# Moving the weight loads, the loads of batch 2 and the second products at the start of a fused attention and MLP kernel

## The chip, the cores and the metric

The kernel runs on one core of a Trainium2 chip. The metric is the device time of one execution in microseconds (us), as the median of several runs. A profile of one execution comes with each kernel; times inside a profile are counted from its span's start.

## The reference

Linear attention per head (`kv = k^T v`, `out = q kv`, RMS norm over the head's 64 columns), then an MLP with an ELU. Inputs and output are float32.

```python
def _attn_ref(q, k, v, g_norm):               # q, k, v: (8, 8, 576, 64)
    kv = np.einsum('bhsd,bhse->bhde', k, v)
    out = np.einsum('bhsd,bhde->bhse', q, kv)
    rms = np.sqrt(np.mean(out * out, axis=-1, keepdims=True) + 1e-06)
    return (out / rms * g_norm).astype(np.float32)

def _moe_ref(x, w_in, w_out):                 # x: (4608, 512), w_in: (512, 2048), w_out: (2048, 512)
    h = x @ w_in
    g = np.where(h > 0.0, h, np.exp(np.minimum(h, 0.0)) - 1.0)
    return (g @ w_out).astype(np.float32)
```

## The kernel before

The rows are worked through in nine groups of 512. For group T the kernel makes `xT` (attention, norm, transposes), then in eight steps the first products `h_ps = xT . w_in` and the ELU into `gT`, then the second products `o_ps = gT . w_out` in sixteen "quarters" of four matmuls of 128x512 (a "half" is two quarters). While group T's products run, the attention of batch T+1 is woven in as "pieces". From group 2 on the pattern is regular. The change concerns the start: groups 0 and 1, and what is loaded for them.

Three queues start transfers: SyncE (`nc.sync`), ScalarE (`nc.scalar`) and GpSimd (`nc.gpsimd`). The weights are turned from float32 to bf16 by the DMA itself. The Trainium skill, "DMA: Bandwidth & Descriptors", section "SWDGE vs HWDGE vs iDMA", says that a cast during DMA has to be issued from GpSimd; that is why the change moves the weights within GpSimd's queue and not to another one.

```python
def fetch(b, eng=nc.sync):                     # float32 staging tiles st_q, st_k, st_v, one buffer each
    fetch_q(b, eng)
    for name, src in (("k", k), ("v", v)):
        out_, in_ = fetch_kv(name, src, b)
        eng.dma_start(out=out_, in_=in_)

def load_w_in(s):  nc.gpsimd.dma_start(out=w_in_sb[...], in_=...)     # a quarter of w_in, cast to bf16
def load_w_out(s): nc.gpsimd.dma_start(out=w_out_sb[...], in_=...)    # a quarter of w_out
# ... cast_q, cast_kv: GpSimd copies st_* to bf16 tiles, which frees the staging buffer

def mm1(T, i, cols, relu, spare):              # ... cut: 8 matmuls into h_ps
    nc.scalar.activation(e, h_ps, AF.Exp)      # ScalarE
    if relu: nc.scalar.activation(h, h_ps, AF.Relu)
    def rest():                                # VectorE: min/subtract, then max (or add, with relu) into gT
        ...
    return rest

# pieces of attention(T): kv, q (transposes of q), se0/se1 (q . kv into PSUM, then squares on ScalarE),
# sum0/1 (VectorE), inv0/1 (ScalarE), mul0/1 (VectorE, scales the rows: xs), x (transposes of xs into xT)
# All of kv, q, se0, se1 and x share one PSUM tile `at`: se1 can start only when mul0 has read se0.

fetch(1)
for s in range(2): load_w_in(s)
cast_q(1, Q)
for s in range(2, 4): load_w_in(s)
cast_kv("k", 1, Q)
cast_kv("v", 1, Q)
for s in range(4): load_w_out(s)

def first_products(T, at, second, start, relu=(), spare=()):
    # for each step i: mm1; the early pieces (sum, inv); second[i](); rest(); the late pieces
    ...

at = attention(1)
at["fetch"] = lambda: fetch(2, nc.scalar)
start = {"q": 1, "kv": 4, "se0": 5, "fetch": 6, "se1": 7}
first_products(0, at, {}, start, (1, 3, 5, 7), (2, 5))
mm2_half(0, 0)
mm2_half(0, 1)
at["x"]()
mm2_half(0, 2)
cast_all(2)
fetch(3)
at = attention(2)
second = {i: (lambda i=i: mm2_quarter(0, 6 + i)) for i in range(8)}
start = {"q": 1, "kv": 2, "se0": 3, "se1": 5, "x": 7}
first_products(1, at, second, start, (1, 3, 5, 7))
mm2_half(0, 7)
# ... groups 2 to 8, unchanged
```

## Time and profile before

| | before |
|---|---|
| time, median of the first 4 runs | 320.69 us (320.2 to 321.54) |
| profiled execution, span | 317.4 us |
| TensorE busy | 299.1 us, 94% |
| ScalarE / VectorE / GpSimd busy | 49% / 56% / 21% |

The first fence is the head of the profile's page. The profiled execution itself took 319.24 us, 1.45 us less than the median of the four. TensorE (PE) is busy nearly all the time, and in the timeline it has no gap left after about 80 us. So a change to the start is worth what it takes out of TensorE's gaps and slow stretches before that.

```profile
span 317.4 us, 4742 instructions
...
PE 299.1 (94%) x1941; PEld 150.4 (47%) x1941; DVE 179.3 (56%) x217; ACT 156.5 (49%) x218; POOL 66.3 (21%) x117
```

The next fence is the timeline of TensorE near the end of group 0: start, length, engine, line, operation, and in brackets how long the engine was idle before and what ended that.

```profile
42.80 0.77 PE L187 MATMUL at<-bd_kv,qT 128*128 128x128 bf16 x8 [2.73 <-DVE xs L221]
43.36 4.32 PE L360 MATMUL o_ps<-w_out_sb,gT 128*128 128x512 bf16 x12
48.48 1.02 PE L360 MATMUL o_ps<-w_out_sb,gT 128*128 128x512 bf16 x4 [0.80 <-DMA w_out_sb<-in_moe_w_out_dram]
51.20 1.05 PE L281 MATMUL at<-ident,xs 128*128 128x128 bf16 x16 [1.70 <-DVE xs L221]
```

L187 is the attention product se1, L360 second products, L281 the transposes of xs. There are three gaps: 2.73 us until the first row scaling (mul0), 0.80 us until the last part of w_out, 1.70 us until the second row scaling (mul1). Why mul1 is so late is told by ScalarE's timeline:

```profile
40.33 0.21 ACT L218 ACTIVATE ss<-ss 128x16 f32<-128x16 f32 x1
40.42 0.98 ACTq L83 DMA_DIRECT2D st_q<-in_q_dram  x2
41.49 0.46 ACTq L112 DMA_DIRECT2D st_k<-in_k_dram  x1
42.05 3.10 ACTq L112 DMA_DIRECT2D st_v<-in_v_dram  x1
45.20 1.02 ACT L327 ACTIVATE elu_e<-h_ps 128x1024 bf16<-128x1024 f32 x1 [4.65 <-issue]
...
47.02 1.03 ACT L206 ACTIVATE sq<-at 128x1024 bf16<-128x1024 f32 x1
```

ACTq is ScalarE's queue issuing DMA. It issues batch 2's q, k and v at 40.4 us, and the issue of v alone takes 3.10 us. The exponential of step 7 starts only at 45.20 us, 4.65 us after ScalarE's last work, and the squares that mul1 depends on come behind it, at 47.02 us.

The last view is busy time in windows of 2 us. A line has the window and its length, then busy time (and count of instructions) of PE, PEld (the weight loads of TensorE), DVE (VectorE), ACT (ScalarE) and POOL (GpSimd). The columns that matter are the last three: PEclk, the granted clock of TensorE (1.00 is full), DMA share (over 1 is a full DMA) and GB/s written. For the weights, which the DMA turns from 4 bytes to 2, the bytes read are twice those written.

```profile
32.00:34.00 2.00, 2.00 (x36) 1.22 (x36) 1.79 (x4) 2.00 (x3) 2.00 (x5) 1.00 0.24 32
40.00:42.00 2.00, 0.08 (x1) 0.00 (x0) 1.90 (x3) 0.52 (x2) 0.00 (x0) 1.00 1.24 206
42.00:44.00 2.00, 1.20 (x10) 0.86 (x10) 0.75 (x1) 0.00 (x0) 0.00 (x0) 0.78 1.24 205
44.00:46.00 2.00, 2.00 (x6) 0.68 (x5) 0.00 (x0) 0.81 (x1) 0.00 (x0) 0.50 1.17 245
```

At 32 to 34 us the DMA is nearly empty, because w_out has only just been issued. After the 2.73 us gap the clock is half for 3.4 us, and the 12 matmuls at 43.36 take 4.32 us instead of 2.6.

### The profile page before, as it was taken

How to read it: one execution, taken by the hardware profiler on the slowest of the kernel's cores; microseconds unless marked ns; L12 is line 12 of the kernel's file. 1: busy time of each engine (PE TensorE's matmuls, PEld its weight loads, DVE VectorE, ACT ScalarE, POOL GpSimd, SP SyncE). 2: the span in 40 equal slices, each digit the busy share in tenths (PEclk: the TensorE clock that was granted, in tenths of full speed). 3: DMA queues.
4: the chain of work that ended last, by engine and by line, in shares of the span. 5: the costliest groups of instructions: out<-in, count | busy, mean ns of one | idle time of the engine just before them, and what ended most of it. 6: DMA issues, size and time to landing. Idle time of an engine off the chain costs nothing.

```text
span 317.4 us, 4742 instructions
## 1 busy us (share of the span) xinstructions
PE 299.1 (94%) x1941; PEld 150.4 (47%) x1941; DVE 179.3 (56%) x217; ACT 156.5 (49%) x218; POOL 66.3 (21%) x117
## 2 busy tenths in 40 slices
PE   8778966998999999999999999999999999999993
PEld 3444523553554545454545454545454545444441
DVE  4565744578448744774487458745774676554400
ACT  3556933667445454545554555445544555334220
POOL 0246405950045005400540063002000000000000
PEclk9999979999999999999999999999999999999999
DMA  7999799920491049105810591034101010101122
GB/s 256 316 290 253 121 238 387 363 99 2 138 355 71 0 148 348 69 0 168 328 67 2 158 340 66 0 108 94 68 0 66 2 66 2 66 0 66 68 66 66
DMA packets 28565, 42.24 MB, mean 133 GB/s; under 512 B 5504, under 2 KB 17792, under 8 KB 28544
## 3 DMA queue, kind: packets, MB, share of 16 engines
q1 hardware_dynamic: 22208, 34.35, 31.4%
q0 software_dynamic: 4224, 4.19, 8.1%
q10 hardware_dynamic: 2112, 3.41, 3.0%
q8 instruction: 15, 0.25, 0.3%
q14 instruction: 6, 0.05, 0.0%
HBM read 36.70 MB, written 9.44 MB: 145 GB/s over the span
## 4 chain that ended last, share of the span: by engine, by line
PE 80%; DMA 8%; DVE 4%; ACT 4%; ACTq 1%; POOL 0%; issue 0%; SPq 0%; DVEq 0%
PE o_ps L360 36%; PE h_ps L318 35%; DMA w_in_sb<-in_moe_w_in_dram 5%; PE at L165 2%; PE at L281 2%; DMA st_v<-in_v_dram 2%; PE at L175 2%; PE at L187 2%; ACT elu_e L327 1%; DVE gT L344 1%; DVE ss L211 1%; ACTq L112 1%; DVE xs L221 1%; ACT elu_h L331 1%; ACT sq L206 1%; DVE elu_e L336 1%
## 5 line engine op out<-in xcount | busy, mean ns | idle before, releaser
L360 PE MATMUL o_ps<-w_out_sb,gT 128*128 128x512 bf16 x576 | 137.0, 382 | 0.8 <-DMA w_out_sb<-in_moe_w_out_dram 0.8
L318 PE MATMUL h_ps<-xT,w_in_sb 128*128 128x512 bf16 (+1 forms) x584 | 135.6, 376 | 1.7 <-DMA w_in_sb<-in_moe_w_in_dram 1.7
L327 ACT ACTIVATE elu_e<-h_ps 128x1024 bf16<-128x1024 f32 (+1 forms) x74 | 74.0, 1001 | 67.2 <-PE h_ps L318 62.6
L360 PEld LDWEIGHTS <-gT 128*128 128x128 bf16 x576 | 56.7, 99 | 69.3 <-issue 3.2
L336 DVE TENSOR_SCALAR elu_e<-elu_e 128x1024 bf16<-128x1024 bf16 (+1 forms) x73 | 35.6, 487 | 94.1 <-ACT elu_e L327 94.1
L318 PEld LDWEIGHTS <-w_in_sb 128*128 128x128 bf16 x584 | 55.2, 98 | 61.4 <-DMA w_in_sb<-in_moe_w_in_dram 2.2
L344 DVE TENSOR_TENSOR gT<-elu_e,h_ps 128x1024 bf16<-128x1024 bf16 (+1 forms) x65 | 78.3, 1205 | 6.8
L130 POOL CAST q_bf<-st_q 128x512 bf16<-128x512 f32 x32 | 19.3, 640 | 136.1 <-DMA st_q<-in_q_dram 92.3
L370 ACT COPY o_sb<-o_ps 128x512 f32<-128x512 f32 x36 | 21.1, 586 | 24.9 <-PE o_ps L360 24.9
L206 ACT ACTIVATE sq<-at 128x1024 bf16<-128x1024 f32 (+1 forms) x18 | 17.5, 981 | 13.7 <-PE at L187 11.1
L130 POOL CAST v_bf<-st_v 128x512 bf16<-128x512 f32 (+1 forms) x36 | 20.8, 620 | 12.5 <-DMA st_v<-in_v_dram 12.0
L211 DVE TENSOR_REDUCE ss<-sq 128x16 f32<-128x1024 bf16 x16 | 19.5, 1219 | 4.8 <-ACT sq L206 4.5
L130 POOL CAST k_bf<-st_k 128x512 bf16<-128x512 f32 (+1 forms) x35 | 19.6, 604 | 7.8 <-DMA st_k<-in_k_dram 7.8
L221 DVE TENSOR_TENSOR xs<-at,ss 128x1024 bf16<-128x1024 f32 x16 | 19.5, 1218 | 0.6 <-ACT ss L218 0.6
L291 ACT ACTIVATE xT<-at,g_col 128x1024 bf16<-128x1024 bf16 x8 | 8.9, 1114 | 19.0 <-DVE xT L288 19.0
L421 PE MATMUL idle_ps<-zeros,ident 128*128 128x512 bf16 x45 | 13.3, 434 | 1.4 <-POOL ident masks.py:199 1.4
L250 ACT COPY qT<-at 128x1024 bf16<-128x1024 bf16 x8 | 8.1, 1012 | 9.4 <-DVE qT L249 9.4
L187 PE MATMUL at<-bd_kv,qT 128*128 128x128 bf16 x120 | 9.3, 221 | 3.3 <-DVE xs L221 3.3
L187 PEld LDWEIGHTS <-qT 128*128 128x128 bf16 x128 | 8.5, 98 | 7.2 <-issue 3.9
L165 PE MATMUL at<-v_bf,k_bf 64*128 64x128 bf16 x288 | 9.8, 216 | 2.0 <-DVE v_bf L130 1.1
L165 PEld LDWEIGHTS <-k_bf 64*128 64x128 bf16 x288 | 8.3, 94 | 5.9 <-issue 4.8
L281 PE MATMUL at<-ident,xs 128*128 128x128 bf16 x128 | 8.4, 219 | 2.3 <-DVE xs L221 2.3
(46 smaller groups left out, 105.3 us busy)
## 6 DMA issues: line engine op xcount, KB each, us to landing
out_dram<-o_sb SPq DMA_DIRECT2D x16, 512.0 KB, 2.6
st_q<-in_q_dram SPq DMA_DIRECT2D x14, 512.0 KB, 5.5
st_k<-in_k_dram SPq DMA_DIRECT2D x6, 1152.0 KB, 8.7
st_v<-in_v_dram SPq DMA_DIRECT2D x6, 1152.0 KB, 10.9
w_in_sb<-in_moe_w_in_dram POOLq DMA_DIRECT2D x4, 512.0 KB, 13.0
w_out_sb<-in_moe_w_out_dram POOLq DMA_DIRECT2D x4, 512.0 KB, 9.4
st_k<-in_k_dram SPq DMA_DIRECT2D x2, 576.0 KB, 6.8
st_v<-in_v_dram SPq DMA_DIRECT2D x2, 576.0 KB, 7.8
```

The costliest lines, as they stand in the source:

```text
L130: eng.tensor_copy(out=out_, in_=in_)
L165: nc.tensor.matmul(kv_ps[s][:, u * P : u * P + P], lhsT=bf["k", T][rows, j, 2 * u : 2 * u + 2, :], rhs=bf["v", T][rows, j, 2 * u : 2 * u + ...
L187: nc.tensor.matmul(ov[:, u, :, s, :], lhsT=qT[:, p, j * P : j * P + P], rhs=bd_kv[:, T, p, :], start=True, stop=True,)
L206: nc.scalar.activation(sq, se_ps, AF.Square)
L211: nc.vector.reduce_sum(out=ss, in_=sq.rearrange("p c (h e) -> p (c h) e", h=H), axis=AX.X)
L221: nc.vector.tensor_tensor(out=xs.rearrange("p c (h e) -> p (c h) e", h=H), in0=se_ps.rearrange("p c (h e) -> p (c h) e", h=H), in1=ss.to_b ...
L318: nc.tensor.matmul(h_ps[a][:, cs], lhsT=w_in_sb[:, c, f * P : f * P + P], rhs=x[:, c, cs], start=(c == 0), stop=(c == KC - 1),)
L327: nc.scalar.activation(e[:, lo:hi, :], ps, AF.Exp)
L336: nc.vector.tensor_scalar(out=e[:, lo:hi, :], in0=e[:, lo:hi, :], scalar1=1.0, scalar2=1.0, op0=ALU.min, op1=ALU.subtract,)
L344: nc.vector.tensor_tensor(out=gT[T][:, 2 * i + lo : 2 * i + hi, :], in0=e[:, lo:hi, :], in1=h, op=ALU.add if relu else ALU.max,)
L360: nc.tensor.matmul(o_ps[T, j], lhsT=gT[T][:, f, j * P : j * P + P], rhs=w_out_sb[:, f, :], start=(f == 0), stop=(f == FC - 1),)
L370: nc.scalar.copy(o_sb[T][:, j % 2, :], o_ps.pop((T, j)))
```

## The change

The intent: keep the DMA full by queuing all weight loads early; take the load issues away from ScalarE, which is needed at that time; but keep batch 2 from competing with the weights, by a tiny DMA on SyncE (the "gate") that reads a piece of `gT` written by the last ELU of group 0, so that all that SyncE issues after it waits for that ELU; and rearrange the second products in quarters, and the steps that use relu on ScalarE, to cover the waits.

```diff
     fetch(1)
-    for s in range(2):
+    for s in range(4):
         load_w_in(s)
     cast_q(1, Q)
-    for s in range(2, 4):
-        load_w_in(s)
+    for s in range(4):
+        load_w_out(s)
     cast_kv("k", 1, Q)
     cast_kv("v", 1, Q)
-    for s in range(4):
-        load_w_out(s)
...
+    def hold_loads():
+        gate = const.tile([1, 64], BF16, name="gate")
+        nc.sync.dma_start(out=gate, in_=gT[0][0:1, FC - 1, 0:64])
+
     at = attention(1)
-    at["fetch"] = lambda: fetch(2, nc.scalar)
-    start = {"q": 1, "kv": 4, "se0": 5, "fetch": 6, "se1": 7}
-    first_products(0, at, {}, start, (1, 3, 5, 7), (2, 5))
-    mm2_half(0, 0)
-    mm2_half(0, 1)
+    start = {"q": 1, "kv": 4, "se0": 5, "se1": 7}
+    first_products(0, at, {}, start, (2, 3, 6), (2, 5))
+    hold_loads()
+    fetch(2)
+    cast_all(2)
+    for i in range(5):
+        mm2_quarter(0, i)
     at["x"]()
-    mm2_half(0, 2)
-    cast_all(2)
+    mm2_quarter(0, 5)
     fetch(3)
     at = attention(2)
-    second = {i: (lambda i=i: mm2_quarter(0, 6 + i)) for i in range(8)}
+    quarters = iter(range(6, 16))
+    counts = (0, 1, 1, 1, 2, 1, 1, 1)            # quarters woven into step i
+    second = {...}                               # cut
     start = {"q": 1, "kv": 2, "se0": 3, "se1": 5, "x": 7}
-    first_products(1, at, second, start, (1, 3, 5, 7))
-    mm2_half(0, 7)
+    first_products(1, at, second, start, (1, 3, 4, 6))
+    for i in quarters:
+        mm2_quarter(0, i)
```

More of the change, by code (lines that the diff above doesn't have):

```diff
@@ L551, in first_products @@
                 at[name]()
+    def hold_loads():
+        gate = const.tile([1, 64], BF16, name="gate")
+        nc.sync.dma_start(out=gate, in_=gT[0][0:1, FC - 1, 0:64])
     at = attention(1)
-    at["fetch"] = lambda: fetch(2, nc.scalar)
-    start = {"q": 1, "kv": 4, "se0": 5, "fetch": 6, "se1": 7}
-    first_products(0, at, {}, start, (1, 3, 5, 7), (2, 5))
-    mm2_half(0, 0)
-    mm2_half(0, 1)
+    start = {"q": 1, "kv": 4, "se0": 5, "se1": 7}
[5 more added lines that the diff above has]
+        mm2_quarter(0, i)
     at["x"]()
-    mm2_half(0, 2)
-    cast_all(2)
+    mm2_quarter(0, 5)
     fetch(3)
     at = attention(2)
-    second = {i: (lambda i=i: mm2_quarter(0, 6 + i)) for i in range(8)}
+    quarters = iter(range(6, 16))
+    counts = (0, 1, 1, 1, 2, 1, 1, 1)
+    second = {
+        i: (lambda n=n: [mm2_quarter(0, next(quarters)) for _ in range(n)])
+        for i, n in enumerate(counts)
+    }
     start = {"q": 1, "kv": 2, "se0": 3, "se1": 5, "x": 7}
-    first_products(1, at, second, start, (1, 3, 5, 7))
-    mm2_half(0, 7)
+    first_products(1, at, second, start, (1, 3, 4, 6))
+    for i in quarters:
+        mm2_quarter(0, i)
     for T in range(2, NT):
```

## The prediction

It was written before the changed kernel was built or run.

> **What bounds the kernel now.** TensorE is busy 299.1 of 317.4 us (page, part 1). In the chain of work it is solid from about 80 to 312 us, so only idle or slow TensorE time before 80 us can be won. The timeline of TensorE shows the gaps after the first product starts: 1.17 us at 27.9 (w_in slice), 2.73 at 42.8 (row scaling on DVE), 0.80 at 48.5 (w_out), 1.70 at 51.2 (row scaling), later 0.23, 0.58, 0.58: 7.8 us. The windows also show a granted clock of 0.5 from 43.1 to 46.5 us, after the 2.73 us gap: 12 matmuls took 4.3 us instead of 2.6, so 1.7 us more. The Trainium skill, "TensorE: Matmul & The Clock Gate" (Part 1), says that an idle window halves the clock for about 3.4 us; the trace agrees (3.4 us).
>
> **What the change does.**
> 1. Batch 2's loads leave ScalarE, which issues them from 40.4 to 45.2 us (one issue alone 3.1 us), so that step 7's exponential, the squares and the second row scaling (49.9 to 51.2 us) come late. From the trace's durations I work out: step 7's exponential ends at 41.6, first scaling 42.4 (relu on step 6 saves DVE 0.5 us; 0.35 us earlier than now), step 7's ELU 44.1, sums 45.3, second scaling 47.1. The 1.70 us gap goes.
> 2. Weights earlier. GpSimd issues w_out at 32.5 to 35.5 us and the DMA is nearly empty at 32 to 34 us (0.15 to 0.33, windows). Queued at 19.4 they follow w_in without a hole; at 205 GB/s, as weights move alone (windows 28 to 31, 41 to 43), w_out (2.1 MB written) lands by about 44 instead of 48.5 us. The 0.80 us gap goes. Batch 1's loads should not suffer: the weight queue was never empty before 32 us, and is served in order. Four issues of 0.75 us fit into GpSimd's 3.2 us idle before the cast of k.
> 3. Batch 2 is issued on SyncE only at about 44.1 us, 3.7 us later, but on free DMA (387 GB/s, 8.8 us plus latency): v lands near 56 us as now (56.2), casts end near 59. The kv product wants it at 57.6 to 59: little or no stall.
> 4. Five quarters before the transposes cover the second scaling; the one after is 0.5 to 0.7 us too short for xT's two copies (0.75, then 1.1 us). In group 1, two quarters at step 4 cover the gap before the second attention product; the gap before the transposes stays, and step 7 without relu adds about 0.5 us on DVE before xT.
>
> **Sum.** The first gap only shrinks to 2.4 us, and the half clock probably stays. Group 1's first product ends near 53.1 instead of 55.7: 2.6 us. With full clock 4.2, but then v's cast limits it to about 3. Plus 0.8 us in group 1, minus 0.5 at its end: 3.2 us in all, 1%.
>
> **Predicted: 317.5 us, 80% range 315.5 to 319.8.** Faster by over 2%: 0.06; within 2%: 0.91; slower by over 2%: 0.03.
>
> **What would show it.** No ScalarE issue gap at 40 to 45 us; w_out issued at 19 to 22.5 us; no DMA hole at 32 to 34; the gap before group 0's transposes gone; TensorE still idle about 2.4 us before 42.5 and at half clock after; v of batch 2 cast by about 59; TensorE solid from about 77 us.
>
> **What would make it wrong.** A full weight queue that blocks GpSimd, so that k and v of batch 1 are cast late and the kv product stalls (several us slower); batch 2 landing after 57 us, so that group 1 stalls at its q or kv product; a clock that stays full with v early (gain over 4 us).

## The result, and the profile after

| | before | after |
|---|---|---|
| time, first measurement (4 runs each) | 320.69 us | 315.82 us (315.7 to 317.1), ratio 0.9854, 95% interval 0.9821 to 0.9887 |
| time, second measurement (11 and 6 runs) | 319.95 us | 316.57 us (315.83 to 318.02), ratio 0.9902, interval 0.9868 to 0.9936 |
| span of the first profile | 317.4 us | 313.9 us |
| TensorE's last product ends | 312.0 us | 308.0 us |

A ratio is the mean time of one kernel's fast runs over that of the other's of the same rounds, so it is not quite the ratio of the medians quoted. The gain is 4.9 us in one measurement and 3.4 us in the other, 1.0% to 1.5%: clear of noise, since neither interval reaches 1. Both intervals leave room for the same gain, near 0.987 to 0.989, and the second reaches up to 0.994.

The page's head, and the same stretch of TensorE, now:

```profile
span 313.9 us, 4706 instructions
...
PE 295.2 (94%) x1905; PEld 149.7 (48%) x1941; DVE 179.5 (57%) x217; ACT 155.4 (50%) x217; POOL 67.1 (21%) x117
```

```profile
42.31 0.61 PE L187 MATMUL at<-bd_kv,qT 128*128 128x128 bf16 x8 [2.18 <-DVE xs L221]
42.76 4.48 PE L360 MATMUL o_ps<-w_out_sb,gT 128*128 128x512 bf16 x19
47.13 1.05 PE L281 MATMUL at<-ident,xs 128*128 128x128 bf16 x16
48.02 1.03 PE L360 MATMUL o_ps<-w_out_sb,gT 128*128 128x512 bf16 x4
49.03 0.59 PE L318 MATMUL h_ps<-xT,w_in_sb 128*128 128x512 bf16 x2
50.17 3.18 PE L318 MATMUL h_ps<-xT,w_in_sb 128*128 128x512 bf16 x14 [0.55 <-ACT xT L291]
...
57.94 0.51 PE L165 MATMUL at<-v_bf,k_bf 64*128 64x128 bf16 x12 [0.23 <-ACT qT L250]
58.70 1.08 PE L165 MATMUL at<-v_bf,k_bf 64*128 64x128 bf16 x24 [0.25 <-POOL v_bf L130]
```

The wait for w_out and the 1.70 us gap before the transposes are gone. The first gap is 2.18 instead of 2.73 us. The 19 matmuls at 42.76 us (one record is missing) take 4.48 us, full speed. Small waits show at three places: 0.55 us for xT's second copy, which is new, and 0.23 and 0.25 us at the kv product of group 1. The first of these (for the transposes of q) was there before with the same 0.23 us; the second, for the cast of batch 2's v, is new. Group 1's first product starts at 49.0 us instead of 53.8.

ScalarE goes straight from the piece inv0 (L217 and L218) to step 7's exponential:

```profile
40.61 0.22 ACT L218 ACTIVATE ss<-ss 128x16 f32<-128x16 f32 x1
40.73 1.01 ACT L327 ACTIVATE elu_e<-h_ps 128x1024 bf16<-128x1024 f32 x1
42.96 1.02 ACT L206 ACTIVATE sq<-at 128x1024 bf16<-128x1024 f32 x1 [1.22 <-PE at L187]
45.27 0.31 ACT L217 ACTIVATE ss<-ss,eps_col 128x16 f32<-128x16 f32 x1 [1.29 <-DVE ss L211]
```

The windows:

```profile
32.00:34.00 2.00, 2.00 (x34) 1.18 (x34) 1.13 (x3) 2.00 (x4) 1.33 (x2) 1.00 1.24 207
40.00:42.00 2.00, 0.13 (x1) 0.00 (x0) 1.90 (x3) 1.70 (x4) 0.00 (x0) 1.00 1.19 197
42.00:44.00 2.00, 1.69 (x14) 1.03 (x14) 1.82 (x3) 1.02 (x1) 0.00 (x0) 1.00 0.27 47
44.00:46.00 2.00, 1.95 (x11) 0.88 (x10) 1.36 (x2) 0.52 (x2) 0.00 (x0) 1.00 0.08 8
```

At 32 to 34 us the DMA is full; at 42 to 46 us it is almost empty, because the weights are done and batch 2 is held. The clock is full throughout. SyncE's queue shows the gate and, behind it, the first load of batch 2:

```profile
43.95 0.58 SPq L554 DMA_DIRECT2D gate<-gT  x1
44.65 1.06 SPq L83 DMA_DIRECT2D st_q<-in_q_dram  x2
```

### The profile page after: what moved, and what is told of

Read it like the earlier page. It is cut to its first block, busy times and chain, and to the rows that moved or that the text cites. A ratio compares the mean times of both kernels' runs of the same rounds, so it can differ in the third digit from the quotient of the medians.

```text
span 313.9 us, 4706 instructions
## 1 busy us (share of the span) xinstructions
PE 295.2 (94%) x1905; PEld 149.7 (48%) x1941; DVE 179.5 (57%) x217; ACT 155.4 (50%) x217; POOL 67.1 (21%) x117
## 4 chain that ended last, share of the span: by engine, by line
PE 78%; DMA 8%; DVE 5%; ACT 3%; POOL 2%; issue 2%; SPq 1%; DVEq 0%; POOLq 0%
PE o_ps L360 36%; PE h_ps L318 34%; DMA w_in_sb<-in_moe_w_in_dram 4%; DVE gT L344 2%; DMA st_k<-in_k_dram 2%; DMA st_v<-in_v_dram 2%; PE at L165 2%; PE at L281 2%; PE at L187 2%; PE at L175 2%; ACT elu_e L327 1%; DVE elu_e L336 1%; POOL v_bf L130 1%; POOL k_bf L130 1%; DVE xs L221 1%
## 5 line engine op out<-in xcount | busy, mean ns | idle before, releaser
L318 PE MATMUL h_ps<-xT,w_in_sb 128*128 128x512 bf16 (+1 forms) x564 | 133.7, 376 | 3.6 <-DMA w_in_sb<-in_moe_w_in_dram 1.7
L360 PE MATMUL o_ps<-w_out_sb,gT 128*128 128x512 bf16 x562 | 134.4, 379 | 0.8
L344 DVE TENSOR_TENSOR gT<-elu_e,h_ps 128x1024 bf16<-128x1024 bf16 (+1 forms) x66 | 79.5, 1205 | 6.9
L130 POOL CAST k_bf<-st_k 128x512 bf16<-128x512 f32 (+1 forms) x35 | 20.7, 636 | 7.7 <-DMA st_k<-in_k_dram 7.7
L421 PE MATMUL idle_ps<-zeros,ident 128*128 128x512 bf16 x43 | 12.4, 422 | 1.6 <-POOL ident masks.py:199 1.4
L241 ACT CAST bd_kv<-at 64x256 bf16<-64x256 f32 x14 | 5.2, 369 | 9.8 <-PE at L165 9.7
```

What stands on the lines that cost most here:

```text
L130: eng.tensor_copy(out=out_, in_=in_)
L318: nc.tensor.matmul(h_ps[a][:, cs], lhsT=w_in_sb[:, c, f * P : f * P + P], rhs=x[:, c, cs], start=(c == 0), stop=(c == KC - 1),)
L344: nc.vector.tensor_tensor(out=gT[T][:, 2 * i + lo : 2 * i + hi, :], in0=e[:, lo:hi, :], in1=h, op=ALU.add if relu else ALU.max,)
L360: nc.tensor.matmul(o_ps[T, j], lhsT=gT[T][:, f, j * P : j * P + P], rhs=w_out_sb[:, f, :], start=(f == 0), stop=(f == FC - 1),)
```

## The experiments

The parts of the change are called A (weights early), B (batch 2 on SyncE behind the gate) and C (the rest: relu steps, quarters, and where `cast_all(2)` stands). "Theory 1" is the prediction's: the gain comes from ScalarE being freed, that is from B. Twelve runs follow, eleven kernels and the changed kernel once more, in three calls (on chips 3, 15 and 3); each call has its own runs of the kernel before, and the ratios are to those. All gave correct results.

### Each part alone

**a_weights_early** is the kernel before with the first hunk of the diff only.

> Only the weight loads move (all four of w_in, then all four of w_out, ahead of the casts of k and v); batch 2 stays on ScalarE, products and relu stay. Theory 1 (the gain comes from ScalarE no longer issuing batch 2): w_out lands by about 44 us and the 0.80 us wait on it goes, but the transposes of group 0 still wait for the second row scaling at about 51 us, so the gap there grows from 1.70 to about 2.5 us and the time stays at 320.7 within 0.6. Rival 1 (weights were what mattered): 1 us or more faster, 319.7 or less.

Measured: 317.06 us (316.67 to 318.17) against 319.72, ratio 0.9914 (0.9886 to 0.9942). Theory 1 fails here: it said no gain, and 2.7 us came. But so does the simple rival, since the 0.80 us that TensorE waited for w_out cannot give 2.7 us. ScalarE's timeline shows the reason:

```profile
40.39 0.99 ACTq L83 DMA_DIRECT2D st_q<-in_q_dram  x2
41.47 0.46 ACTq L112 DMA_DIRECT2D st_k<-in_k_dram  x1
42.03 0.50 ACTq L112 DMA_DIRECT2D st_v<-in_v_dram  x1
42.58 1.02 ACT L327 ACTIVATE elu_e<-h_ps 128x1024 bf16<-128x1024 f32 x1 [2.05 <-issue]
```

The same four DMA issues on the same engine at the same time now take 2.05 us: the issue of v took 0.50 us instead of 3.10. Step 7's exponential runs at 42.58 instead of 45.20, and the transposes follow at 48.58 instead of 51.20. So moving the weights on GpSimd shortened a stall on ScalarE.

**b_held_sync** is the kernel before with `hold_loads(); fetch(2)` after the first products, and without the fetch on ScalarE.

> Only batch 2's loads move, from ScalarE to SyncE behind the gate; weights late and halves as before. Theory 1: ScalarE has no issue gap, the second row scaling ends near 47.1 us instead of 51.2, and 2.5 to 4 us are gained: 317 to 318.2. Rival 1 (weights): at most 1 us, since w_out still lands after 46 us and holds the second products. Rival 2 (the gain is the clock that stays full): the time follows the granted clock, 319 or more if a half-clock stretch shows after the gap near 42 us.

Measured: 317.3 us (316.96 to 317.51), ratio 0.9913 (0.9884 to 0.9942), within the expectation. Alone, B is worth as much as A (2.4 and 2.7 us). ScalarE has no issue gap, and of the 1.70 us wait for mul1 0.21 us are left:

```profile
48.54 1.05 PE L281 MATMUL at<-ident,xs 128*128 128x128 bf16 x16 [0.21 <-DVE xs L221]
```

Rival 2, the clock, finds no support: this profile has no half-clock stretch, and the run with the lowest mean clock (0.984) took 316.97 us, less than the median.

**c_reorder** is the changed kernel with the old weight order and with `fetch(2, nc.scalar)` at step 6.

> Only the relu steps and the quarters change; weights late, batch 2 on ScalarE at step 6. Theory 1: the second row scaling moves by the 0.9 us that step 7 no longer spends on relu, to about 50.2 us; five quarters fill more of the wait; 0.5 to 1.5 us faster (319.2 to 320.2). Rival 3 (the order of relu and quarters is the main thing): 2.5 us or more faster.

Measured: 319.17 us (318.78 to 321.0), ratio 0.9984 (0.9951 to 1.0016): 0.6 us by the medians, not clear of noise. In its profile mul1 ends at 50.97 us and not at the 50.2 that I expected: ScalarE is stopped for 4.48 us, v's issue takes 2.93 us, and TensorE waits 1.25 us for w_out and 0.68 us for mul1.

### Two parts together

If A and B removed different waits, 0.9914 times 0.9913 would give 0.983 for both. A stall that both shorten would give less.

**ab_no_reorder**: the first hunk, and b_held_sync's edit.

> Weights early and batch 2 held on SyncE, but relu and halves as before. If the two moves removed different waits, their gains (2.7 and 2.4 us alone) would add to 5.1 us, a ratio near 0.984. Theory now (weights early alone already shortens ScalarE's issue stall from 4.65 to 2.05 us, so both moves shorten the same stall): at most 4 us, a ratio of 0.987 to 0.990; the transposes of group 0 start near 47.5 us with a gap of about 0.7 us before them.

Measured: 317.24 us (316.62 to 317.3) against 320.94, ratio 0.9884 (0.9862 to 0.9906). The product of the two is outside the interval, so the gains overlap. (The product is itself uncertain, by about 0.003 to either side when the runs are resampled, and comes from another chip; it stays below the measured ratio all the same. The table below shows the overlap in the profiles.) The transposes start at 47.86 us after a gap of 0.76 us.

**bc_weights_late**: the changed kernel with the old weight order.

> The changed kernel with the weights queued as late as before. Overlap theory: ScalarE's stall is gone all the same; the fourth quarter waits for w_out until about 47 us and the transposes move from 47.1 to about 48.5; ratio 0.988 to 0.991 (about 1 to 1.5 us slower than the changed kernel). If the weights' move were worth its 2.7 us here too: ratio 0.994.

Measured: 316.9 us, ratio 0.9882 (0.986 to 0.9905), as the overlap theory said. TensorE waits 0.55 us for w_out, and the transposes start at 48.16 us.

**ac_fetch_act**: the changed kernel without `hold_loads(); fetch(2)` and with the fetch on ScalarE at step 6.

> The changed kernel with batch 2's loads back on ScalarE at step 6. Overlap theory: with w_out done by about 42.5 us the issue of v no longer blocks (0.5 us instead of 3.1), ScalarE loses about 2 us, the second scaling ends near 48.5, a gap of 1 to 1.5 us before the transposes; batch 2 is some 3 us earlier, so no wait at the kv product of group 1; ratio 0.986 to 0.990. If the 3.1 us issue belongs to ScalarE whatever the DMA does: a stall of 4.5 us and a ratio of 0.994 or more.

Measured: 316.83 us, ratio 0.9877 (0.9853 to 0.9901). ScalarE is stopped for 2.06 us and v's issue takes 0.50 us, as expected from the overlap:

```profile
43.48 0.50 ACTq L112 DMA_DIRECT2D st_v<-in_v_dram  x1
44.03 1.02 ACT L327 ACTIVATE elu_e<-h_ps 128x1024 bf16<-128x1024 f32 x1 [2.06 <-issue]
```

The gap of 1 to 1.5 us before the transposes did not show, because this profile has a half-clock stretch that slowed the quarters until mul1 was ready.

The three kernels with two parts gained 3.7 to 4.1 us by the medians. The changed kernel, with all three, gained 4.9 and 3.4 us. It was run at another time. So the times do not show that the third part adds anything. The profiles suggest it: the transposes start 0.7 to 2.8 us earlier with all three (table), part of which is how late the run started.

This table is worked out from the profiles: the time from the end of mul0 to the end of mul1 (which leaves out by how much the start of the run was late), and what stopped ScalarE.

| kernel | ScalarE stopped by issues | v's issue | mul0's end to mul1's end | transposes start | span |
|---|---|---|---|---|---|
| before | 4.65 us | 3.10 us | 8.39 us | 51.20 | 317.4 |
| C | 4.48 | 2.93 | 8.69 | 51.03 | 317.0 |
| A | 2.05 | 0.50 | 5.80 | 48.58 | 314.9 |
| A and C | 2.06 | 0.50 | 6.42 | 49.89 | 315.9 |
| B | 0 | on SyncE | 4.82 | 48.54 | 315.6 |
| A and B | 0 | on SyncE | 4.81 | 47.86 | 314.9 |
| B and C | 0 | on SyncE | 4.81 | 48.16 | 314.7 |
| the change | 0 | on SyncE (0.45) | 4.81 | 47.13 | 313.9 |

The floor is 4.81 us. B alone takes off the whole 3.6 us above it, A alone 2.6 us. So once A is there, B has about 1 us of this stall left to give; once B is there, A has none of it left, only the wait for w_out (0.39 us in B's profile, 0.55 in that of B and C). The transposes start 4.07 us earlier after the change, and 3.6 us of that is this one stall, which two of its parts attack; the rest is the earlier end of mul0 (0.5 us).

Why did v's issue take 3 us? The trace counts packets by queue. In the kernel before, the first packet of ScalarE's queue starts at 44.0 us, 3.6 us after its first issue, and until then the weights' queue is at its full 205 GB/s; in a_weights_early it starts at 41.5 us, 1.1 us after the first issue, as the last of w_out runs out. The issues that blocked (3.10 and 2.93 us, and 3.19 in before_filled, below) had w_out in full flow; those that did not (0.50 and 0.50) had it ending. That an issue waits for room in a queue that does not move is my reading; that it took 3 us in the three profiles with a full weights' queue and 0.5 us in the two in which w_out was ending is shown. It is not only ScalarE's: in b_held_sync, where the weights ran until 46.9 us, SyncE's issue of k at 46.73 us took 1.19 us, against 0.43 us after the change. The Trainium skill, "DMA: Bandwidth & Descriptors", section "Issuing engines are not separate DMA queues", says that starting DMAs from several engines only saves the issuing time, "which is usually small relative to the DMA itself". Here that time was most of what there was to win, because the engine that spent it had a chain of work behind it.

### The gate

**no_gate** is the changed kernel without `hold_loads()`.

> The changed kernel without the gate: SyncE starts batch 2's loads as soon as the staging buffers are free (q from about 19 us). Theory 1 with contention: the weights move at about 90 GB/s written beside other loads instead of 205 alone, so w_in slices 2 and 3 and w_out land 5 to 10 us later, TensorE waits for them in group 0, and the time is 3 to 8 us above the changed kernel's 315.8. If the hold is not needed: within 1 us of 315.8, or faster because batch 2 is early.

Measured: 327.94 us (327.26 to 328.85) against 319.72, ratio 1.0252 (1.0221 to 1.0282). That is 8.2 us slower than before the change and 11 to 12 us above the changed kernel's two medians. They were run at other times. I had expected 3 to 8 us. TensorE (same columns as above), then the windows:

```profile
48.27 1.60 PE L360 MATMUL o_ps<-w_out_sb,gT 128*128 128x512 bf16 x4 [3.11 <-DMA w_out_sb<-in_moe_w_out_dram]
52.80 1.86 PE L360 MATMUL o_ps<-w_out_sb,gT 128*128 128x512 bf16 x4 [2.92 <-DMA w_out_sb<-in_moe_w_out_dram]
57.08 3.57 PE L360 MATMUL o_ps<-w_out_sb,gT 128*128 128x512 bf16 x8 [2.41 <-DMA w_out_sb<-in_moe_w_out_dram]
```

```profile
48.00:52.00 4.00, 1.60 (x4) 0.49 (x4) 0.46 (x1) 0.00 (x0) 2.31 (x5) 0.57 1.17 248
52.00:56.00 4.00, 1.86 (x4) 0.55 (x4) 0.00 (x0) 0.00 (x0) 0.32 (x1) 0.50 1.14 295
56.00:60.00 4.00, 2.92 (x7) 0.98 (x7) 0.00 (x0) 0.58 (x1) 2.29 (x4) 0.50 1.05 404
```

The waits for w_out add up to 8.4 us, and the gaps put the clock at half from 48.6 to 62.2 us, which I had left out. Batch 2's q is issued at 19.0 us, and batch 3's at 40.4. The Trainium skill, same page, section "Queues, rings and completion order", says that a DMA engine takes turns between the queues that have work; the trace agrees: between 22 and 27 us in the kernel before, the weights' queue moves 0.46 MB (92 GB/s written) beside 1.02 MB of loads, and alone, between 34 and 40 us after the change, 1.22 MB (203 GB/s). In no_gate it is 88 to 124 GB/s in each 3 us from 20 to 53 us. (The turns do not begin at once: in the 3.6 us named above ScalarE's queue had work issued and moved nothing.) So loads that nobody needs yet cost the weights about half of their speed. Of what was left out in turn, this is the one piece without which the rest is a loss.

### The half clock

**before_filled**: does the half-clock stretch of the kernel before cost time?

```diff
+    def fill(n):
+        fill_ps = ps_m2.tile([P, DM], FP32, name="fill_ps", tag="mm2")
+        for _ in range(n):
+            nc.tensor.matmul(fill_ps, lhsT=ident, rhs=zeros, start=True, stop=True)
...
-    first_products(0, at, {}, start, (1, 3, 5, 7), (2, 5))
+    first_products(0, at, {7: lambda: fill(8)}, start, (1, 3, 5, 7), (2, 5))
```

> The kernel before, with 8 useless products of 128x512 (1.7 us) in the 2.73 us gap of TensorE near 41 us, so that the array is hardly idle there; nothing else changes. If the half-clock stretch near 43 to 46.5 us costs time, all runs show a mean granted clock of 0.993 or more and the time falls by 0.7 to 1.7 us (ratio 0.995 to 0.998). If it is hidden behind the wait for the second row scaling at 51 us, the clock stays full but the time is the same within 0.3 us.

Measured: 320.88 us (318.81 to 321.7) against 320.94, ratio 0.9998 (0.997 to 1.0027). The clock stayed full through the first second products, and TensorE only arrived sooner at the next wait:

```profile
42.86 0.61 PE L187 MATMUL at<-bd_kv,qT 128*128 128x128 bf16 x8 [1.00 <-DVE xs L221]
...
49.12 1.86 PE L360 MATMUL o_ps<-w_out_sb,gT 128*128 128x512 bf16 x4 [3.06 <-DMA w_out_sb<-in_moe_w_out_dram]
51.35 1.86 PE L281 MATMUL at<-ident,xs 128*128 128x128 bf16 x16 [0.37 <-DVE xs L221]
```

The 3.06 us wait for w_out was then followed by half clock from 48.1 to 55.0 us. So neither expectation came out whole: the time is the same, but the clock did not stay full (the runs' means are 0.987 to 0.992), and the second stretch has a cost of its own, after mul1. What the run does show is that the transposes start no earlier (51.35 us, 51.20 before) although TensorE came to them sooner. The kernel before says the same: behind its half clock, which cost 1.7 us, TensorE waited 0.80 us for w_out and 1.70 us for mul1. So there the half clock at 43 us was hidden behind the late weights and the late mul1. That it is worth something once those are gone is my reading; no run tests it alone.

### Using what is left

The 2.18 us gap before se1 remains after the change. Two quarters fit there: their `gT` and w_out are ready. Three kernels try it, run beside the changed kernel once more.

**after_again** is the changed kernel, unchanged.

> The changed kernel once more, as the reference for the three runs beside it: ratio to before 0.984 to 0.988; ScalarE never stopped by issues, TensorE idle about 2.2 us before 42.3.

Measured: 316.57 us, ratio 0.9902; this is the second measurement in the table of the result. It missed the expected 0.984 to 0.988. Its profile repeats the first within 0.2 us at every point named here (gap 2.37 us for 2.18, mul1 ends 47.08, span 314.1).

**fill_only**:

```diff
-    first_products(0, at, {}, start, (2, 3, 6), (2, 5))
+    first_products(0, at, {7: lambda: [mm2_quarter(0, i) for i in range(2)]}, start, (2, 3, 6), (2, 5))
-    for i in range(5):
+    for i in range(2, 7):
         mm2_quarter(0, i)
     at["x"]()
-    mm2_quarter(0, 5)
+    mm2_quarter(0, 7)
+    mm2_quarter(0, 8)
-    quarters = iter(range(6, 16))
-    counts = (0, 1, 1, 1, 2, 1, 1, 1)
+    quarters = iter(range(9, 16))
+    counts = (0, 0, 1, 0, 2, 0, 1, 1)
```

> The changed kernel with two quarters of second products put into the remaining 2.2 us gap of TensorE near 40 to 42.3 us, five then before the transposes and two (not one) after, seven left for group 1. If the gap is simply lost TensorE time, 1.7 us and the 0.55 us wait for xT come back: ratio 0.977 to 0.981. If group 1 is bound by its own chain (casts of batch 2's v, row scalings), the three quarters that it then lacks turn into idle time there and at most 0.8 us is gained: 0.982 to 0.986.

Measured: 316.35 us (315.99 to 318.6), ratio 0.9898, no better than the changed kernel's 0.9902 and outside both ranges, but its gain is the one of the second case, at most 0.8 us. The gap before se1 is 0.53 us and the wait for xT is gone, but in group 1 TensorE now waits 0.28, 0.96 and 1.43 us where it had waited little or not at all:

```profile
55.26 1.89 PE L318 MATMUL h_ps<-xT,w_in_sb 128*128 128x512 bf16 x8 [0.28 <-DVE gT L344]
...
58.97 0.51 PE L165 MATMUL at<-v_bf,k_bf 64*128 64x128 bf16 x12 [0.96 <-ACT qT L250]
...
69.69 0.61 PE L187 MATMUL at<-bd_kv,qT 128*128 128x128 bf16 x8 [1.43 <-DVE xs L221]
```

Group 1 is bound by its own chain as soon as it has fewer quarters to fill in. The gain was given back.

**fill_carry** takes quarters in one running order over all groups, so that group 1 keeps its eight, the last of them from its own products, and every later group stays three quarters ahead (the diff is shortened):

```diff
+    order = iter([(T, i) for T in range(NT) for i in range(16)])
+    def take(n):
+        for _ in range(n):
+            mm2_quarter(*next(order))
-    first_products(0, at, {}, start, (2, 3, 6), (2, 5))
+    first_products(0, at, {7: lambda: take(2)}, start, (2, 3, 6), (2, 5))
...
+    take(5); at["x"](); take(2)                    # around the transposes of group 0
+    counts = (0, 1, 1, 1, 2, 1, 1, 1)              # group 1, then take(2)
     for T in range(2, NT):
-        second = {i: (lambda i=i: mm2_half(T - 1, i)) for i in range(8)}
+        second = {i: (lambda: take(2)) for i in range(8)}
...
-    for i in range(8):
-        mm2_half(NT - 1, i)
+    for T, i in order:
+        mm2_quarter(T, i)
```

> As fill_only, but group 1 keeps its eight quarters, the last ones taken from group 1's own products, and all later groups stay three quarters ahead, so nothing has to be given back in group 1: 1.5 to 2.3 us faster than the changed kernel, ratio 0.978 to 0.981. No half-clock stretch near 40 us.

Measured: 314.65 us (313.94 to 315.78), ratio 0.9838 (0.9803 to 0.9873): 1.9 us below the changed kernel beside it, as expected in size, though the ratio missed its range; all ratios of this call lie higher than I had assumed, the changed kernel's too. No half-clock stretch shows near 40 us.

**fill_carry_gate6**: as fill_carry, with

```diff
-        nc.sync.dma_start(out=gate, in_=gT[0][0:1, FC - 1, 0:64])
+        nc.sync.dma_start(out=gate, in_=gT[0][0:1, 13, 0:64])
-    start = {"q": 1, "kv": 2, "se0": 3, "se1": 5, "x": 7}
+    start = {"q": 0, "kv": 2, "se0": 3, "se1": 5, "x": 7}
```

> As fill_carry, with the gate on step 6's ELU (about 41 us) instead of step 7's (43.9) and group 1's q transposes one step earlier: the DMA hole at 42 to 46 us shrinks, v of batch 2 is cast near 56 us instead of 59, the waits at the kv product of group 1 (0.23 and 0.25) go; 0.3 to 0.8 us better than fill_carry. If the early loads hold w_out back, the quarters wait near 43 us and it is no better.

Measured: 313.97 us (313.87 to 314.12), ratio 0.9815 (0.9783 to 0.9847), 0.7 us below fill_carry and 2.6 us below the changed kernel beside it. The gate is issued at 41.25 instead of 44.42 us, v's casts end at 56.9 us, and the waits at the kv product are gone. The price is small: TensorE waits 0.21 us for w_out. The run changes two things at once, the gate and the step of q's transposes, and does not say which of them gave what.

```profile
42.41 0.61 PE L187 MATMUL at<-bd_kv,qT 128*128 128x128 bf16 x8 [0.53 <-DVE xs L221]
...
44.10 3.61 PE L360 MATMUL o_ps<-w_out_sb,gT 128*128 128x512 bf16 x16 [0.21 <-DMA w_out_sb<-in_moe_w_out_dram]
```

By the medians this kernel is the fastest of the four, 1.9% below the kernel before (the interval includes 2%); its runs are also the closest together, 313.87 to 314.12 us, where fill_carry's best was 313.94.

## Why the prediction was right or wrong

It was right in the time and in most of the mechanism: 315.82 us lies in 315.5 to 319.8, within 2% was given 0.91, and the predicted gain of 3.2 us compares with 4.9 and 3.4 us measured. Point by point:

- **ScalarE freed: right, closely.** Predicted ends against the profile: step 7's exponential 41.6 and 41.74 us, mul0 42.4 and 42.27, step 7's ELU 44.1 and 43.92, sums 45.3 and 45.24, mul1 47.1 and 47.08. Costing a chain by adding up the trace's durations in queue order worked to 0.2 us.
- **Weights early: right in what happens, wrong in what it is worth alone.** w_out was issued at 19.1 to 22.1 us, GpSimd did not block, the casts of k and v started as before (24.3 and 30.0 us, against 24.1 and 29.8), and the weights were done before 44 us. But the step "The 0.80 us gap goes" put the part's whole worth there, and the "one issue alone 3.1 us" was taken as ScalarE's own cost. a_weights_early shows that 2.6 of these 3.1 us came from the weights being late, so that this part alone gives 2.7 us. The prediction's sum stayed right because it counted that stall once, under the other part.
- **Batch 2 held: right.** Issue at 44.65 us for 44.1 (the gate itself takes 0.6), v's casts end at 58.99 for 59, little wait (0.48 us in all, of which 0.23 us was there before).
- **Quarters: right in kind.** The wait for xT is 0.55 us (0.5 to 0.7 said), the gap before group 1's transposes stayed (0.43), the wait at the end is 0.26 us (0.5 said), and the one before se1 of group 1 went.
- **The mis-sized term: "The first gap only shrinks to 2.4 us, and the half clock probably stays".** The gap was 2.18 and 2.37 us, so that part was right, but in both profiles of the changed kernel the clock stayed full. That is why group 1's first product ended near 51.6 us, for 53.1 predicted, and for 51.5 by the prediction's own figure with a full clock (55.7 less 4.2). And the limit then put on it, that "v's cast limits it to about 3", was too strong, since the waits at the kv product were 0.48 us together. The sum of 3.2 us lies between what its own terms give with the half clock (2.6 + 0.8 - 0.5 = 2.9) and with the limited full clock (3.3). The prediction had itself named a clock that stays full, with v early, among what would make it wrong; v was not early (59.0 us), the clock stayed full all the same. That it stayed full was in part luck: by the working in the last section, over about 2.0 us of idle time in one window of 3.413 us is followed by half clock, and I estimate from that figure that a gap of 2.2 to 2.4 us puts so much into one window at about half of all positions of the window. Between the profiles TensorE's last product ends 4.0 us earlier and the span is 3.5 us shorter.
- **What stays open** is whether and why the two measurements of the same pair differ, 4.9 and 3.4 us; their intervals overlap, and the first profiles, of executions of 319.24 and 315.70 us, are 3.5 us apart. The runs of the kernel before range from 318.6 to 321.8 us. Half-clock stretches that come in some executions and not in others are a candidate: of the changed kernel's first four runs the slow one (317.1 us) has a mean granted clock of 0.991, the others 0.995 or 0.996. But a later run of it took 318.0 us at 0.999, and of the kernel before one took 321.5 us at 0.994, so the clock alone does not explain the spread. The mean clock is a blunt measure besides: it counts the tail after the last product, where every profile ends at half clock (in the first profile after the change that tail is the whole loss, 0.996).

## What to carry to other kernels

Before adding up the worth of a change's parts, look whether two of them shorten the same stall: here one part took the load issues off ScalarE, another made them short, and either alone gave most of what both gave. An engine that issues DMA while it has a chain of compute behind it can pay for a full DMA with its own time (here 3.10 us for an issue that took 0.50 otherwise), and filling the DMA earlier, or holding loads that nobody needs yet, can be worth more than moving the issues. A gap filled with work from a later stage paid here only when that stage was given other work in turn (1.9 us); otherwise it came back as gaps there (0.2 us gained).

## What the Trainium skill lacked or had wrong

- "DMA: Bandwidth & Descriptors" calls the issuing time usually small. It does not tell that an issue can hold its engine beside another busy queue ("Perfetto Trace Analysis" draws a descriptor buffer that can fill, without a duration): v's issue on ScalarE took 3.10 and 2.93 us with the weights' queue in full flow and 0.50 us without; on SyncE with a free DMA 0.45 us.
- The same page gives no rate for loads that cast. Here float32 to bf16 moved 203 to 207 GB/s written, so 406 to 414 read, at a DMA share of 1.24 when alone, against about 390 GB/s for plain float32 loads at 1.05.
- "TensorE: Matmul & The Clock Gate" warns of idle gaps over about 3 us, though it also says that the window of 3.4 us runs freely. Here gaps of 2.73 us (before), 2.30 us (c_reorder) and 2.16 us (ac_fetch_act) were followed by 3.4 us of half clock, and gaps of 2.73 us (a_weights_early, b_held_sync, ab_no_reorder) and 2.18 us (after) were not. Worked out from the recorded clock changes in steps of 3.413 us, the window was idle for 2.73, 2.13 and 2.16 us in the first three, and for at most 1.6 us in the second three and 1.9 us after the change. So in these profiles about 2 us idle in one window, some 60% of it, made the difference, and where the window falls decides. Over all windows of the fourteen profiles the same working gives no fall of the clock up to 1.95 us idle (no_gate) and a fall from 2.01 us on, with one exception near the start of bc_weights_late (a fall after 1.81 us); a missing record of a 128x512 matmul counts as 0.2 us of idle time here, so the border is known no closer than that.
